# Splitting the first block's loads over two DMA queues in a fused attention and feed-forward kernel

## The chip, the cores and the metric

The kernel runs on one core of a Trainium2 chip. The metric is the device time of one execution in microseconds. TensorE (PE) multiplies matrices, VectorE (DVE), ScalarE (ACT) and GpSimd (POOL) work element by element, and SyncE (SP) issues DMAs. ACT can issue DMAs too, from its own queue, in the order of its other instructions. Each engine takes its instructions in order.

## The reference

```python
def _attn_ref(q, k, v):                      # 4 x 8 heads x 576 x 64
    scores = scale * np.matmul(q, k.transpose(0, 1, 3, 2))
    rel = pos[:, None] - pos[None, :]
    mask_local = (rel >= 0) & (rel < stride)           # heads 0 to 3, stride 32
    mask_strided = (rel >= 0) & (pos[None, :] % stride == pos[:, None] % stride)   # heads 4 to 7
    scores = np.where(masks[None, :, :, :], scores, -1000000000.0)
    ...                                      # softmax over the keys
    return np.matmul(attn, v)

def _moe_ref(x, w_gate, w_val, w_out, rms_g):          # x 2304 x 512, d_ff 1536
    xn = x / rms * rms_g
    g = xn @ w_gate
    silu = g * (1.0 / (1.0 + np.exp(-g)))
    return silu * (xn @ w_val) @ w_out

def _moe2_ref(x, w_a, w_b, w_out):
    return (x @ w_a) * (x @ w_b) @ w_out
```

The output is `_moe2_ref` of `_moe_ref` of the attention's output.

## The kernel before

**Tiling.** The 576 positions are cut into 6 blocks of 96, so a block has 4 x 96 = 384 rows of the feed-forward input. For each block t the attention makes the input (four tiles xx of 128 channels x 384, each a hi part and a lo part in fp32r, so that three matmuls, hi x hi, hi x lo and lo x hi, stand for one in full precision). Then 12 chunks fc of 128 hidden units follow: 12 matmuls into g_ps, 12 into v_ps (L481 to L483), the gate on DVE and ACT, a hi and a lo part of the hidden tile (hl, L506 and L507), and 12 matmuls into y. Block t + 1's attention runs on DVE, ACT and POOL beside block t's matmuls. After block 5 the second feed-forward network follows (L854 to L925).

**Weights.** They come from DRAM as 64-bit words, 512 KB for each third of a chunk (gate, value, out), into tiles gv_raw. A conversion makes 32-bit floats of them: two steps on ACT (L137 and L142) and one on DVE (L145, out cz), all called words steps here, then a hi cast on ACT and a lo subtraction on DVE or POOL (L150 and L151). `convert1(fc)` converts a chunk's gate and value thirds, and all this is done during block 0 alone; later blocks load the converted out weights again.

**Block 0's attention.** Heads 0 to 3 are local: scores on PE (qk, L296), mask (smask, L314), row maximum (lmax, L323), exponentials on ACT (lexp, L336), normalisation (lnorm, L348), transposes (pt, L358) with copies on ACT (ptc, L368), product with the values (pv, L378). They go in three groups 0, 1, 2. Heads 4 to 7 are strided: products on POOL (sqk, L248) that DVE sums (L251), a small softmax (ssub, sexp, snorm), products with the values on POOL (spv, L281), again summed by DVE (L284). POOL has two buffers for its products. pvc and xstc make xx and the squares (L387, L432, lo part L389), rms and rinv the norm. Twenty matmuls on idle data (WARM) and 36 later ones keep PE at work ahead of the first real ones.

**What sets the order.** `LOADS0` and `STEPS0` are lists of names that are called one after the other; a scheduler then orders each engine's instructions, keeping to dependences and to `tc.issue_after` bounds. `GATES` names, for the conversion of chunk 0, 1, 2, 3 and all later ones, which steps of block 0 it has to be issued after (pvr is a sum over values, snorm the strided normalisation, xhi and xlo the last hi and lo part of xx). A DMA waits for its semaphore lane; there are eight, used in turn. All input loads of the kernel before are issued by SP.

Of the kernel before, what the change touches and what calls it, by code (L numbers as in the profile page):

```python
# [37 lines left out]

LOADS0 = "la0 lq ls0 cst la1 lb0 lvl1 lb1 lvl0 lv0"
STEPS0 = ("sqk00 sqk01 sqk02 qk0 qk1 qk2 smask0 lmax0 lexp0 smask1 lmax1 lexp1 smask2 ssub sexp "  # L40
# [5 lines left out]
         "norm pvm snorm sqr",  # L46
         "pvr snorm xhi",
         "snorm sqr sqrt xhi",
# [28 lines left out]
@with_exitstack  # L77
def fused_kernel(ctx: ExitStack, tc: tile.TileContext, qtl, ktl, vl, qs, ks, vs, cst, w1, w2, out):

# [107 lines left out]
    def attention(t, pool, psum, banks):  # L187
# [4 lines left out]
        st = {}  # L192
        steps = {}

        def bank():
# [5 lines left out]
        def load_local(hf, first=False):  # L201

            def f():
                q_t = st["q", hf] = pool.tile([128, 8 * PB], F32, tag="q", name="q_t", bufs=2)
                k_t = st["k", hf] = pool.tile([128, 4, 128], F32, tag="k", name="k_t", bufs=2)
                n = 512 if first else 8 * PB
                nc.sync.dma_start(q_t[:, :n], qtl[t, hf, :, :n])
                nc.sync.dma_start(k_t, ktl[t, hf])
            return f

        def load_rest(hf):
            def f():
                nc.sync.dma_start(st["q", hf][:, 512:], qtl[t, hf, :, 512:])
            return f
# [10 lines left out]
        def load_q():  # L225
            q_t = pool.tile([128, 4, 3, D], F32, tag="qx", name="qs_t", bufs=1)
            nc.sync.dma_start(q_t, qs[:, :, 3 * t:3 * t + 3, :])
            st["qs"] = q_t
# [3 lines left out]
        def load_kv(src, key, g):  # L232
            def f():
                k_t = pool.tile([128, KX], F32, tag="kv", name="kv_t", bufs=KB)
                k_t = k_t[:, :G * L * D].rearrange("p (g n d) -> p g n d", g=G, d=D)
                nc.sync.dma_start(k_t, src[:, heads(g), :L, :])
                st[key, g] = k_t
# [185 lines left out]
        def sqrt_set():  # L423

            with tc.issue_after(st["exp"].ins):
                nc.scalar.activation(scr, eps_sb, AF.Sqrt)
# [88 lines left out]
    const1 = cpool.enter_context(tc.tile_pool(name="const1", bufs=1))  # L515
    cst_sb = const1.tile([128, 388], F32, name="cst_sb")
    ident = cst_sb[:, 0:128]
    mask_a = cst_sb[:, 128:320].rearrange("p (a k) -> p a k", a=2)
    mask_b = cst_sb[:64, 320:384].rearrange("p (a k) -> p a k", a=1)
    g_sb = cst_sb[:, 384:388]  # L520
    pts = [const1.tile([128, 4, 2, PB], F32, name=f"pt{hf}") for hf in range(2)]
# [46 lines left out]
    s0 = attention(0, pool, psum, itertools.cycle(["att", "y0", "y1", "y2", "y3"]))  # L568
    s0["cst"] = lambda: nc.sync.dma_start(cst_sb, cst)
    for n in LOADS0.split():  # L570
        s0[n]()
    load_units(NFC)
    load_late([(NFC - 4, 2), (NFC - 3, 2)])
# [410 lines left out]
def _layout(inputs):  # L984
# [17 lines left out]
    def st(a):  # L1002
        return a[:, 4:].reshape(B, 4, NM, W, D)
    r["qs"] = c(st(q).transpose(0, 3, 1, 2, 4).reshape(128, 4, NM, D))
    r["ks"] = c(st(k).transpose(0, 3, 1, 2, 4).reshape(128, 4, NM, D))
    r["vs"] = c(st(v).transpose(0, 3, 1, 2, 4).reshape(128, 4, NM, D))

    def ok(rows, n):
        i, j = np.arange(rows)[:, None] % (rows // 2), np.arange(n)[None, :]
        return (j > i) & (j <= i + W), j  # L1010
    cst = np.zeros((128, 388), np.float32)
    cst[:, 0:128] = np.eye(128)
    m, j = ok(128, 96)
    cst[:, 128:224] = np.where(m & (j >= W), BIG, NEG)
    cst[:, 224:320] = np.where(m, BIG, NEG)
    cst[:64, 320:384] = np.where(ok(64, 64)[0], BIG, NEG)
    cst[:, 384:] = np.asarray(inputs["moe_rms_g"]).reshape(NCC, 128).T
    r["cst"] = cst

# [25 lines left out]
```

## Time and profile before

| | us |
|---|---|
| median of 3 runs | 964.13 |
| range of the runs | 962.64 to 965.04 |
| the profiled execution | 965.19 |
| its span, first to last instruction | 963.4 |
| PE busy in the span | 936.9 (97%) |
| DVE, ACT, POOL busy | 624.8, 421.7, 541.8 |

PE's busy time is a share of the span, and says that it is seldom idle. Where it is idle is read from the stretches; what it waits for there, from its waits; and why that comes late, from the timelines of the other engines, following at each step what ended the idle time before an instruction. The granted clock of PE is 1 at 2.4 GHz and 0.5 at 1.2 GHz.

### The profile page before, as it was taken

The page shows a single profiled execution, that of the slowest core. Times are in us where ns is not written, and L with a number is a line of the kernel's source. Part 1 is how long each engine was busy: PE and PEld are TensorE (multiplying, and loading weights), DVE is VectorE, ACT ScalarE, POOL GpSimd, SP SyncE. Part 2 cuts the span into 40 slices and gives each one's busy share as a digit, 9 for nine tenths or more (in the row PEclk, how much of TensorE's full clock was granted, in tenths as well). Part 3 has the DMA queues.
Part 4 walks back from the last instruction along what each step waited for, and adds up shares of the span by engine and source line. Part 5 has one row for each costly group of instructions (what it writes and reads, how often), then busy time and mean ns, then how long its engine had stood idle before and what let it go on. Part 6 is the DMA issues. An engine that isn't in the chain of part 4 may idle for free.

```text
span 963.4 us, 14134 instructions
## 1 busy us (share of the span) xinstructions
PE 936.9 (97%) x5324; PEld 889.0 (92%) x5324; DVE 624.8 (65%) x913; ACT 421.7 (44%) x792; POOL 541.8 (56%) x407
## 2 busy tenths in 40 slices
PE   5998999999999999999999999999999999999998
PEld 4798999999999999999999898999999999999997
DVE  5669867548818895987566378667655655464534
ACT  5987655334433433444555455435425422122110
POOL 3568946458749687969379545654734424123211
PEclk6899999999999999999999999999999999999999
DMA  9964375426534553532788975997993973753701
GB/s 344 408 258 157 110 281 195 159 99 215 175 105 149 174 179 111 177 129 66 270 332 307 358 267 202 369 422 278 359 383 118 341 295 131 290 235 147 259 31 66
DMA packets 57507, 215.55 MB, mean 224 GB/s; under 512 B 5984, under 2 KB 14816, under 8 KB 51808
## 3 DMA queue, kind: packets, MB, share of 16 engines
q1 hardware_dynamic: 57296, 214.53, 61.0%
q8 instruction: 42, 0.69, 0.3%
q14 instruction: 25, 0.20, 0.1%
q10 hardware_dynamic: 144, 0.13, 0.0%
HBM read 172.17 MB, written 42.47 MB: 223 GB/s over the span
## 4 chain that ended last, share of the span: by engine, by line
PE 65%; DVE 7%; POOL 6%; DMA 5%; ACT 4%; issue 4%; SPq 0%; DVEq 0%; ACTq 0%; POOLq 0%
PE o L925 5%; PE o L923 5%; PE o L924 5%; POOL prod L248 4%; DMA raw<-in_w 4%; PE Y L856 4%; PE Y L855 4%; PE Y L854 4%; PE y L482 3%; PE Z L856 3%; PE Z L855 3%; PE Z L854 3%; PE y L483 3%; PE X L854 3%; PE X L856 2%
## 5 line engine op out<-in xcount | busy, mean ns | idle before, releaser
L151 POOL TENSOR_TENSOR hl<-c,hl 128x384 fp32r<-128x384 f32 x72 | 77.4, 1076 | 180.2 <-ACT hl L150 173.6
L248 POOL TENSOR_TENSOR prod<-kv_t,qs_t 128x512 f32<-128x512 f32 (+12 forms) x57 | 107.3, 1903 | 21.5 <-DMA wo<-wod 9.7
L482 PE MATMUL y<-hl,wo 128*128 128x384 f32 x288 | 98.3, 345 | 4.8 <-DVE hl L507 3.7
L281 POOL TENSOR_TENSOR prod<-kv_t,S_t 128x512 f32<-128x512 f32 (+12 forms) x57 | 86.8, 1536 | 22.5 <-issue 8.2
L481 PE MATMUL v_ps<-xx,gv 128*128 128x384 f32 x288 | 97.2, 337 | 1.9 <-DVE sg L760 1.9
L481 PE MATMUL g_ps<-xx,gv 128*128 128x384 f32 x288 | 97.6, 339 | 0.6 <-DVE sg L764 0.6
L482 PE MATMUL v_ps<-xx,gv 128*128 128x384 f32 x288 | 97.6, 339 | 0.0
L483 PE MATMUL v_ps<-xx,gv 128*128 128x384 f32 x288 | 97.2, 338 | 0.0
L483 PE MATMUL g_ps<-xx,gv 128*128 128x384 f32 x288 | 97.1, 337 | 0.0
L482 PE MATMUL g_ps<-xx,gv 128*128 128x384 f32 x288 | 96.8, 337 | 0.0
L861 DVE TENSOR_TENSOR c<-c,Y 128x384 f32<-128x384 f32 x108 | 58.9, 550 | 58.0 <-PE Y L856 53.6
L483 PE MATMUL y<-hl,wo 128*128 128x384 f32 x288 | 95.4, 340 | 0.0
L507 POOL TENSOR_TENSOR hl<-h,hl 128x384 fp32r<-128x384 f32 x60 | 64.9, 1081 | 51.1 <-ACT hl L506 51.0
L284 DVE TENSOR_REDUCE xs_t<-prod 128x64 f32<-128x448 f32 (+17 forms) x57 | 85.9, 1521 | 10.5 <-POOL prod L281 9.4
L481 PE MATMUL y<-hl,wo 128*128 128x384 f32 x288 | 83.7, 342 | 3.7 <-ACT hl L506 2.1
L924 PE MATMUL o<-slab,hl 128*128 128x512 f32 x214 | 83.7, 392 | 0.0
L923 PE MATMUL o<-slab,hl 128*128 128x512 f32 x214 | 83.7, 392 | 0.0
L925 PE MATMUL o<-slab,hl 128*128 128x512 f32 x214 | 82.5, 394 | 0.0
L150 ACT CAST hl<-c 128x384 fp32r<-128x384 f32 x72 | 37.0, 514 | 94.9 <-DVE c L891 94.6
L856 PE MATMUL Y<-slab,form 128*128 128x384 f32 x216 | 73.1, 338 | 0.0
L855 PE MATMUL Y<-slab,form 128*128 128x384 f32 x216 | 73.0, 338 | 0.0
L854 PE MATMUL Y<-slab,form 128*128 128x384 f32 x216 | 73.0, 338 | 0.0
(148 smaller groups left out, 2463.5 us busy)
## 6 DMA issues: line engine op xcount, KB each, us to landing
form<-formd SPq DMA_DIRECT2D x32, 1792.0 KB, 10.6
wo<-wod SPq DMA_DIRECT2D x60, 512.0 KB, 4.1
raw<-in_w SPq DMA_DIRECT2D x40, 512.0 KB, 7.2
gv_raw<-in_w SPq DMA_DIRECT2D x32, 512.0 KB, 10.1
formd<-form SPq DMA_DIRECT2D x6, 1792.0 KB, 7.5
formd<-forms SPq DMA_DIRECT2D x6, 1792.0 KB, 12.5
slab<-x2d SPq DMA_DIRECT2D x24, 384.0 KB, 4.0
wod<-wo SPq DMA_DIRECT2D x12, 512.0 KB, 3.2
```

What stands on the lines that cost most here:

```text
L248: nc.gpsimd.tensor_tensor(pr, st["ks", g][:, :, :n, :], st["qs"][:, heads(g), mm:mm + 1, :].to_broadcast([128, G, n, D]), op=ALU.mult)
L281: st["pvm"] = nc.gpsimd.tensor_tensor(pr, st["vs", g][:, :, :n, :], st["S"][:, heads(g), mm, :n, None].to_broadcast([128, G, n, D]), op=AL ...
L284: st["pvr"] = nc.vector.tensor_reduce(st["xs"][:, mm, heads(g), :], pr.rearrange("p g n d -> p g d n"), axis=X, op=ALU.add)
L481: nc.tensor.matmul(out_ps, w_hi, x_hi, start=start, stop=False)
L482: nc.tensor.matmul(out_ps, w_hi, x_lo, start=False, stop=False)
L483: nc.tensor.matmul(out_ps, w_lo, x_hi, start=False, stop=stop)
L854: nc.tensor.matmul(bank(n), hi, x[p][:, 0, c], start=begins and c == 0, stop=False, skip_group_check=not begins)
L855: nc.tensor.matmul(bank(n), hi, x[p][:, 1, c], start=False, stop=False, skip_group_check=not begins)
L856: nc.tensor.matmul(bank(n), lo, x[p][:, 0, c], start=False, stop=c == 1, skip_group_check=not begins)
L923: nc.tensor.matmul(o, h[:, 0, cols], w[0], start=n == 0, stop=False)
L924: nc.tensor.matmul(o, h[:, 0, cols], w[1], start=False, stop=False)
L925: nc.tensor.matmul(o, h[:, 1, cols], w[0], start=False, stop=n == len(chunks) - 1)
```

## The change

Block 0's loads go into two queues: SP keeps q, the strided queries (qs), the values and the weights, and ACT issues the local keys, the masks, the strided keys (ks), the rest of q's second half and the identity. The constants are split into masks (with the gains, 260 columns) and the identity (128 columns). The first chunk's gate and value thirds (`w0`) are issued ahead of the values. The strided queries, keys and values of block 0 get arrays of their own, in which a partition's data is contiguous. The table that prepares the square root is also to be issued after the strided exponentials. The gate of chunk 2 gets xlo.

```diff
-LOADS0 = "la0 lq ls0 cst la1 lb0 lvl1 lb1 lvl0 lv0"
+LOADS0 = "la0 masks lq ls0 la1 lb0 lb1 w0 cst lvl1 lv0 lvl0"
...
-         "pvr snorm xhi",
+         "pvr snorm xhi xlo",
...
+        second = nc.scalar if t == 0 else nc.sync
...
-                nc.sync.dma_start(k_t, ktl[t, hf])
+                second.dma_start(k_t, ktl[t, hf])
...
-                nc.sync.dma_start(st["q", hf][:, 512:], qtl[t, hf, :, 512:])
+                (second if hf else nc.sync).dma_start(st["q", hf][:, 512:], qtl[t, hf, :, 512:])
...
-            nc.sync.dma_start(q_t, qs[:, :, 3 * t:3 * t + 3, :])
+            nc.sync.dma_start(q_t, qs[t])
...
-                nc.sync.dma_start(k_t, src[:, heads(g), :L, :])
+                if t == 0:
+                    (second if key == "ks" else nc.sync).dma_start(k_t, {"ks": ks0, "vs": vs0}[key])
+                else:
+                    nc.sync.dma_start(k_t, src[:, heads(g), :L, :])
...
-            with tc.issue_after(st["exp"].ins):
+            with tc.issue_after(st["exp"].ins), tc.issue_after(st["sexp"].ins):
                 nc.scalar.activation(scr, eps_sb, AF.Sqrt)
...
-    cst_sb = const1.tile([128, 388], F32, name="cst_sb")
+    cst_sb = const1.tile([128, 128], F32, name="cst_sb")
+    mask_sb = const1.tile([128, 260], F32, name="mask_sb")
...
-    s0["cst"] = lambda: nc.sync.dma_start(cst_sb, cst)
+    s0["masks"] = lambda: nc.scalar.dma_start(mask_sb, masks)
+    s0["cst"] = lambda: nc.scalar.dma_start(cst_sb, cst)
+    s0["w0"] = lambda: load_units(1)
...
-    load_units(NFC)
+    load_units(NFC - 1)
```

What the scheduler makes of it shows at three places. (Line numbers of the new file are 4 to 8 higher: its L340 is L336 of before, L372 is L368, L268 is L264, L391 is L387, L436 is L432, L511 is L507, L783 is L776, L785 is L778, L767 is L760.)

ACT, from the program's start, before:

```order
L336 ACT_TABLE_LOAD
L336 ACTIVATE s_t,lsm<-s_t,lmx 128x96 x8
L137 ACTIVATE gv_raw<-gv_raw 128x512
L142 ACTIVATE cz<-gv_raw 128x512
L368 COPY pt_114<-att 96x8x64
L264 ACTIVATE S_t<-S_t 128x12x3
```

and after:

```order
L209 DMA k_t<-in_ktl 128x512
L574 DMA mask_sb<-in_masks 128x260
L238 DMA kv_t<-in_ks 128x768
L209 DMA k_t<-in_ktl 128x512
L214 DMA q_t<-in_qtl 128x256
L575 DMA cst_sb<-in_cst 128x128
L340 ACT_TABLE_LOAD
L340 ACTIVATE s_t,lsm<-s_t,lmx 128x96 x4
L137 ACTIVATE gv_raw<-gv_raw 128x512
L142 ACTIVATE cz<-gv_raw 128x512
L340 ACTIVATE s_t,lsm<-s_t,lmx 128x96 x4
L137 ACTIVATE gv_raw<-gv_raw 128x512
```

Six DMA issues stand ahead of the table load, and the first third's words steps have moved from behind the second group's exponentials to between the first and the second group's. (The fifth issue waits for the lane of the first, the sixth for that of the masks.)

ACT, around chunk 1's conversion and the first scalings of xx, before:

```order
L142 ACTIVATE cz<-gv_raw 128x1024
L387 ACTIVATE xx<-att,cst_sb 128x384
L432 ACTIVATE sq<-att 128x384
L150 CAST gv<-cz 128x2x512
L387 ACTIVATE xx<-att,cst_sb 128x384
L432 ACTIVATE sq<-att 128x384
L387 ACTIVATE xx<-att,cst_sb 128x384 x2
L137 ACTIVATE gv_raw<-gv_raw 128x1024
```

and after:

```order
L142 ACTIVATE cz<-gv_raw 128x1024
L391 ACTIVATE xx<-att,mask_sb 128x384
L436 ACTIVATE sq<-att 128x384
L391 ACTIVATE xx<-att,mask_sb 128x384
L436 ACTIVATE sq<-att 128x384
L150 CAST gv<-cz 128x2x512
L391 ACTIVATE xx<-att,mask_sb 128x384 x2
L137 ACTIVATE gv_raw<-gv_raw 128x1024
```

The cast of chunk 1 has moved behind the second scaling and its square.

DVE, ahead of the lo part of chunk 5's hidden tile, before:

```order
L778 SCALAR_TENSOR_TENSOR v_ps<-th,v_ps 128x384
L760 SCALAR_TENSOR_TENSOR sg<-g_ps,rinv 128x384
L346 TENSOR_SCALAR lsm<-lsm 64x8
L347 RECIPROCAL lrs<-lsm 64x8
L348 TENSOR_TENSOR s_t<-s_t,lrs 64x512
L251 TENSOR_REDUCE S_t<-prod 128x2x6
L776 TENSOR_TENSOR v_ps<-sg,v_ps 128x384
L145 SCALAR_TENSOR_TENSOR cz<-gv_raw,cz 128x1024
L260 TENSOR_REDUCE smx<-S_t 128x12
L507 TENSOR_TENSOR hl<-v_ps,hl 128x384
```

and after:

```order
L350 TENSOR_SCALAR lsm<-lsm 64x8
L351 RECIPROCAL lrs<-lsm 64x8
L145 SCALAR_TENSOR_TENSOR cz<-gv_raw,cz 128x1024
L352 TENSOR_TENSOR s_t<-s_t,lrs 64x512
L767 SCALAR_TENSOR_TENSOR sg<-g_ps,rinv 128x384
L785 SCALAR_TENSOR_TENSOR v_ps<-th,v_ps 128x384
L145 SCALAR_TENSOR_TENSOR cz<-gv_raw,cz 128x512
L255 TENSOR_REDUCE S_t<-prod 128x2x6
L783 TENSOR_TENSOR v_ps<-sg,v_ps 128x384
L511 TENSOR_TENSOR hl<-v_ps,hl 128x384
```

The words step of 1024 columns has moved from straight ahead of the lo part to seven places ahead, with one of 512 columns behind it, and the gate's last step for this chunk (v_ps<-th,v_ps) has moved closer to the lo part.

## Rows read from the trace of the kernel before

**Rows 1.** Stretches: start:end and length in us; PE, PEld, DVE, ACT, POOL busy; clock, DMA.

```profile
0.00:6.00 6.00, 4.95 (x25) 3.77 (x26) 0.26 (x3) 1.28 (x1) 1.62 (x6) 1.00 0.64 187
9.00:29.50 20.50, 12.80 (x82) 10.20 (x83) 15.46 (x34) 15.30 (x38) 10.48 (x8) 0.50 1.03 407
...
40.00:53.50 13.50, 10.06 (x52) 8.61 (x52) 8.91 (x14) 13.47 (x19) 5.63 (x3) 1.00 1.04 405
...
88.00:91.00 3.00, 0.06 (x1) 0.00 (x0) 3.00 (x3) 1.21 (x3) 1.83 (x1) 1.00 0.27 109
91.00:94.50 3.50, 2.94 (x9) 2.94 (x10) 3.50 (x8) 2.41 (x7) 0.73 (x1) 0.51 0.70 214
...
131.50:963.40 831.90, 823.56 (x4653) 784.84 (x4651) 530.61 (x769) 323.41 (x607) 459.12 (x353) 1.00 0.60 219
```

**Rows 2.** Issue and landing of the first raw weights.

```profile
L111 SPq DMA_DIRECT2D gv_raw<-in_w x1: 581/581/581, 8.2 to 8.2; - x1
...
DMA to landing us min/median/max: 6.3/6.3/6.3
```

**Rows 3.** Timeline of DVE, first 16 us: start, duration, instruction, idle time before it.

```profile
8.25 0.56 DVE L314 SCALAR_TENSOR_TENSOR s_t<-att,cst_sb 128x384 f32<-128x384 f32 x1 [7.17 <-DMA cst_sb<-in_cst]
...
12.36 0.56 DVE L314 SCALAR_TENSOR_TENSOR s_t<-att,cst_sb 128x384 f32<-128x384 f32 x1 [2.05 <-PE att L296]
```

**Rows 4.** Timeline of PE, 5 to 25 us.

```profile
5.29 1.23 PE L296 MATMUL att<-k_t,q_t 128*128 128x96 f32 x8
10.34 3.89 PE L296 MATMUL att<-k_t,q_t 128*128 128x96 f32 x24 [3.82 <-DMA k_t<-in_ktl]
```

**Rows 5.** Timeline of ACT, 9 to 52 us.

```profile
13.54 0.37 ACT L336 ACTIVATE s_t<-s_t,lmx 128x96 f32<-128x96 f32 x1 [2.37 <-DVE lmx L323]
...
14.99 0.64 ACT L137 ACTIVATE gv_raw<-gv_raw 128x512 f32<-128x512 f32 x1
...
16.84 0.58 ACT L368 COPY pt<-att 96x512 f32<-96x512 f32 x1 [0.65 <-PE att L358]
...
18.10 1.28 ACT L426 ACT_TABLE_LOAD   x1
...
25.75 1.14 ACT L142 ACTIVATE cz<-gv_raw 128x1024 uint32<-128x1024 uint16 x1
...
29.29 1.04 ACT L150 CAST gv<-cz 128x1024 fp32r<-128x1024 f32 x1 [1.42 <-DVE cz L145]
...
35.21 0.88 ACT L432 ACTIVATE sq<-att 128x384 f32<-128x384 f32 x2
...
51.43 0.46 ACT L506 CAST hl<-v_ps 128x384 fp32r<-128x384 f32 x1
```

**Rows 6.** Timeline of POOL, 7 to 24 us.

```profile
19.03 1.96 POOL L281 TENSOR_TENSOR prod<-kv_t,S_t 128x256 f32<-128x256 f32 x2 [7.67 <-DVE S_t L273]
22.01 2.46 POOL L281 TENSOR_TENSOR prod<-kv_t,S_t 128x768 f32<-128x768 f32 x1 [1.02 <-DVE xs_t L284]
```

**Rows 7.** Timeline of DVE, 18 to 30 us.

```profile
20.73 0.81 DVE L145 SCALAR_TENSOR_TENSOR cz<-gv_raw,cz 128x512 uint32<-128x512 uint32 x1 [0.72 <-ACT cz L142]
...
21.57 0.36 DVE L284 TENSOR_REDUCE xs_t<-prod 128x256 f32<-128x256 f32 x1
```

**Rows 8.** ACT's one DMA issue, at the kernel's end: duration in ns, start.

```profile
L918 ACTq DMA_DIRECT2D out_dram<-slab x1: 377/377/377, 960.7 to 960.7; - x1
```

**Rows 9.** PE's waits, 33 to 150 us: releaser, us in total, times, longest.

```profile
PE y L482 <- DVE hl L507: 3.7, 2, 3.5
PE v_ps L481 <- DVE sg L760: 1.9, 2, 1.0
PE y L481 <- ACT hl L506: 1.4, 1, 1.4
```

**Rows 10.** Timeline of DVE, 80 to 92 us.

```profile
87.83 3.08 DVE L145 SCALAR_TENSOR_TENSOR cz<-gv_raw,cz 128x1024 uint32<-128x1024 uint32 x1
...
90.97 0.54 DVE L507 TENSOR_TENSOR hl<-v_ps,hl 128x384 fp32r<-128x384 f32 x1
```

More of the change, by code (lines that the diff above doesn't have):

```diff
@@ L77, in fused_kernel @@
 @with_exitstack
-def fused_kernel(ctx: ExitStack, tc: tile.TileContext, qtl, ktl, vl, qs, ks, vs, cst, w1, w2, out):
+def fused_kernel(ctx: ExitStack, tc: tile.TileContext, qtl, ktl, vl, qs, ks, vs, ks0, vs0, masks, cst, w1, w2, out):
     nc = tc.nc
@@ L515, in fused_kernel @@
     const1 = cpool.enter_context(tc.tile_pool(name="const1", bufs=1))
-    cst_sb = const1.tile([128, 388], F32, name="cst_sb")
[L517 to L520, printed above, removed]
+    cst_sb = const1.tile([128, 128], F32, name="cst_sb")
+    mask_sb = const1.tile([128, 260], F32, name="mask_sb")
+    ident = cst_sb
+    mask_a = mask_sb[:, 0:192].rearrange("p (a k) -> p a k", a=2)
+    mask_b = mask_sb[:64, 192:256].rearrange("p (a k) -> p a k", a=1)
+    g_sb = mask_sb[:, 256:260]
     pts = [const1.tile([128, 4, 2, PB], F32, name=f"pt{hf}") for hf in range(2)]
@@ L1003, in st @@
         return a[:, 4:].reshape(B, 4, NM, W, D)
-    r["qs"] = c(st(q).transpose(0, 3, 1, 2, 4).reshape(128, 4, NM, D))
+    r["qs"] = c(st(q).transpose(0, 3, 1, 2, 4).reshape(128, 4, NB, NM // NB, D).transpose(2, 0, 1, 3, 4))
     r["ks"] = c(st(k).transpose(0, 3, 1, 2, 4).reshape(128, 4, NM, D))
     r["vs"] = c(st(v).transpose(0, 3, 1, 2, 4).reshape(128, 4, NM, D))
+    r["ks0"], r["vs0"] = (c(r[n][:, :, :NM // NB]) for n in ("ks", "vs"))
     def ok(rows, n):
@@ L1010, in ok @@
         return (j > i) & (j <= i + W), j
-    cst = np.zeros((128, 388), np.float32)
-    cst[:, 0:128] = np.eye(128)
+    cst = np.zeros((128, 260), np.float32)
     m, j = ok(128, 96)
[L1014 to L1018, printed above, removed]
+    cst[:, 0:96] = np.where(m & (j >= W), BIG, NEG)
+    cst[:, 96:192] = np.where(m, BIG, NEG)
+    cst[:64, 192:256] = np.where(ok(64, 64)[0], BIG, NEG)
+    cst[:, 256:] = np.asarray(inputs["moe_rms_g"]).reshape(NCC, 128).T
+    r["masks"] = cst
+    r["cst"] = np.eye(128, dtype=np.float32)
     def weights(a, b, o):
```

## The prediction

> **What bounds the kernel now.** I read the stages first [rows 1]: the reader is to see that TensorE (PE) is the bound almost everywhere. From 131.5 us to the end it is busy 823.56 of 831.90 us, and past some 200 us the instructions of PE, ACT, DVE and POOL stand in the same order in both programs. So the change can pay only in what stands ahead: the attention of block 0 up to the first real matmul, and the first block's 12 chunks, in which ACT, DVE and POOL convert weights while PE works. Three stretches of [rows 1] show where PE loses time there: 9.00 to 29.50 (12.80 of 20.50 busy, at half clock, 1.2 GHz), 40.00 to 53.50 (10.06 of 13.50) and 88.00 to 91.00 (0.06 of 3.00). PE's waits [rows 9] name the releasers of the last two: sg on DVE, the first hi copy on ACT, and 3.7 us for a lo part on DVE. In 40.00 to 53.50 ACT is busy 13.47 of 13.50 us: there ACT's queue is the bound, and whatever lets ACT reach that stretch sooner moves PE by as much.
>
> Then I followed the chain back from there. ACT's pair of squares (35.21) stands behind a cast that waited 1.42 us for DVE, and that behind the words step at 25.75 [rows 5], which starts when POOL frees a buffer: POOL's third value product at 22.01 [rows 6]. That one waited 1.02 us for a DVE reduce (21.57), which stood behind a words step that had waited 0.72 us for ACT [rows 7]. The first value product (19.03) waited for the strided softmax, which hangs on the local one: DVE idles 7.17 us for the constants [rows 3], PE 3.82 us for the second keys [rows 4], ACT 2.37 us for the second row maximum [rows 5].
>
> **The change part by part.** *Masks.* They leave the large constant load and become the second DMA of ACT's queue. That issue falls at 0.73 plus one issue of 0.38 [rows 8], so about 1.1. The constants were issued at 3.0 and let DVE go at 8.25 [rows 3], 5.2 later; with the same 5.2 the masks are there at 6.3 at the latest, before PE has the first scores (5.29 + 1.23 = 6.52 [rows 4]). So PE becomes the releaser: the first mask step at 6.6 rather than 8.25, a gain of 1.65.
>
> *ACT as an issuer.* Six issues of 0.38 [rows 8] are 2.3 us, and the sixth (the identity) waits for the masks, so ACT is held until about 6.3 + 0.4 = 6.7; behind it is queued ACT's first table load, 1.28 as the later one took [rows 5], ready at 8.0. The first exponentials need the row maximum at 6.6 + 1.18 = 7.8 (mask to exponential took 13.54 - 12.36 = 1.18 [rows 3, 5]). So issuing costs 0.2 of the 1.65; without that cover it would be the whole 3.6.
>
> *Second keys and first raw weights.* The keys are issued fourth on ACT, near 1.9, rather than seventh on SP. Before, PE was let go at 10.34 [rows 4]. The bytes ahead of them are nearly the same, so their gain is what idle DMA time is filled: DMA was busy 64% of the first 6 us [rows 1], 2.2 us idle, and 103% afterwards. Bounds 8.1 and 10.3; I take 9.0, since the first queued transfers are what two issuers fill. PE needs 2.0 us for them (10.34 to 12.36), so the second mask step comes at 11.0 (10.1 to 12.3). DVE's new order puts the first normalisation (0.56, as the like-sized step of [rows 3]) ahead of the second maximum: second exponentials at 11.0 + 0.56 + 1.18 = 12.7 (11.9 to 14.0) for 13.54. ACT's order puts two conversion steps of 0.64 [rows 5] between the first and second exponentials, in the 2.37 us that it waited. They need the first raw weights: before, issued at 8.2, landed 6.3 later at 14.5 [rows 2]; now 960 KB fewer stand ahead, 2.4 us at the 407 GB/s of [rows 1], so 12.1 at the latest and, with all idle time filled, 9.9. I take 11.0: ACT is through at 12.3 and holds nothing. Gain at the second exponentials 0.8 (-0.5 to 1.6). The values move behind the weights: they land about 14, needed at 17.8.
>
> *From there to POOL.* The same steps follow in both orders. The second pair of conversion steps stands where the first pair stood. ACT's wait for PE before its copy (0.65 [rows 5], of which I take 0.4) goes, since the first normalisation is done long before: the first value product at 17.8 for 19.03, gain 1.2. The third product's 1.02 us of waiting shrinks, as the reduce no longer stands behind a words step that waits for ACT, but stands behind three of them: about 0.5 less. Gain 1.7 at the words step of 25.75.
>
> *ACT's order around the first cast.* Now two scalings and two squares stand ahead of the cast, where one of each stood: about 0.9 of the 1.42 us wait is filled (two squares take 0.88 [rows 5], and a scaling has a square's shape). Gain 2.6 at 35.21. The gate on the third chunk (xlo) puts the last two lo parts of the input ahead of the chunk's words steps on DVE; ACT's words steps are late enough (over 1 us behind the scalings) that DVE has time for them: nothing, and a cost of up to 1.1 (the two lo steps, 2 x 0.56) if that cover is gone.
>
> *ACT's order in the bound stretch.* One conversion step of 0.64 now stands ahead of the first hi copy (51.43 [rows 5]), which PE waits for [rows 9]: -0.6. Gain 2.0 (0.7 to 2.8).
>
> *The 3.7 us stall stays.* DVE's steps ahead of that lo part are the same set in another order, and PE stands at the same point of its own work there (96 + 84 + 64 matmuls). So it moves with the rest. After it PE is never idle until 131.5, and the end moves with it.
>
> I deduct 0.1 for PE's squares, which now stand apart. Sum: -1.65 + 0.2 + 0.65 (what DVE's order and the second keys give back, from 1.45 to 0.8) - 0.4 - 0.5 - 0.9 + 0.6 + 0.1 = **-1.9 us**. Against the profiled execution, 965.19 (span 963.4 and 1.8 around it), that is 963.3; that execution lies 1.06 above the median of the runs, so I predict 964.13 - 1.9 = **962.2**.
>
> **The rivals.** (a) *The second queue brings nothing but order.* If the transfers ahead arrive no sooner, second keys come at 10.3, second exponentials at 14.0, 0.5 later than before, the gain at 25.75 falls to 0.4, and at the end to 0.6: **963.5**. For it: DMA is at 103% from 9 us on [rows 1]; against it: the 64% before 6 us. The Trainium skill, "DMA: Bandwidth & Descriptors", section "Issuing engines are not separate DMA queues", says that DMAs of several issuers run on the same 16 engines and that a second issuer saves only issue time, which stands for this case; the row's idle third in the first 6 us speaks against it, and no run here yet shows two queues.
> (b) *The stall at 88 goes.* Before, a words step that took 3.08 us stood straight ahead of the lo part [rows 10]; now other steps do. If that wait vanishes, 3.5 us and half of the 3.5 us at 1.2 GHz that follow it [rows 1], 1.7, come on top: **957.0**; with half the wait gone and no fall of the clock, 1.75 + 1.7 more, **958.7**. Against: DVE's total ahead of the lo part is unchanged, and the words step is slow beside POOL, whose work is unchanged too.
> (c) *Slower: ACT held by the raw weights.* ACT takes its queue in order; the second exponentials now stand behind a step that waits for 512 KB. They come at landing + 1.3, and the end moves by (that - 13.54) less 1.1 (0.4 + 0.5 + 0.9 - 0.6 - 0.1). It turns slower when they land after 13.3. If the two queues share so that they land at 15.5, 1 us after the old time: 16.8 - 13.54 - 1.1 = +2.2, **966.3**. Against: only 12.1 by the bytes ahead.
>
> **How the numbers follow.** Forecast 0.57, (a) 0.16, (b) 0.20, (c) 0.07. The forecast is the likeliest, 962.2, with its own range of 961.4 to 963.5. The range that should hold 8 in 10 reaches into half of (b) and up to the near side of (c): 958.6 to 965.2. About 0.3% is what a measurement of this kernel can tell from no change, 2.9 us: below 961.2 lie (b) and 0.04 of the forecast's edge, 0.23 in all (a little of (b) misses it); above 967.0 some of (c) and orders that go wrong unseen, 0.05; within, 0.72.
>
> **What would show it.** Right: first mask step at 6.5 to 6.8, released by PE; second exponentials near 12.7; first value product near 17.8; words step of the second chunk near 24; ACT busy without a break from about 35.5; the 3 us stall on DVE's lo part near 86; PE's stretch from the second block on unchanged. Wrong: ACT idle on a raw weight between the exponentials (c), the words step of the second chunk after 25 (a), no stall near 86 (b), or a new stall of PE in the first block, which no step here has.

## The result, and the profile after

The changed kernel takes 969.43 us (median of 6 runs, 968.31 to 969.82). The kernel before, run beside it, has 962.35 (6 runs, 961.0 to 965.04). The ratio is 1.0067, 95% interval 1.0052 to 1.0083: about 6.5 us **slower** (7.1 by the medians). The forecast was 962.2, with a range of 958.6 to 965.2, and 5% for slower.

| | before | after |
|---|---|---|
| median, us | 962.35 | 969.43 |
| profiled execution, us | 965.19 (a second one: 962.7) | 969.41 |
| its span, us | 963.4 (960.9) | 967.5 |
| granted clock, mean of the span | 0.986 (0.991) | 0.989 |
| PE, DVE, ACT, POOL busy, us | 936.9, 624.8, 421.7, 541.8 | 937.4, 631.1, 423.6, 538.9 |

The profiled execution of before that the prediction rests on lies 2.8 us above its median, while that of after lies at its median. So before was profiled once more (below, "The kernel before, profiled again"), in an execution of 962.7 us, and what stands behind the first 60 us is compared with that one. DVE is the engine whose busy time grew most, by 6.3 us (5.4 against the second profile).

**The start went as forecast.** The timelines of the changed kernel (start, duration, instruction, idle time before it) begin with what the load part of the change was to bring. First DVE, ACT and PE up to 13 us; these answer to [rows 3 to 5]:

```profile
6.68 0.56 DVE L318 SCALAR_TENSOR_TENSOR s_t<-att,mask_sb 128x384 f32<-128x384 f32 x1 [5.59 <-PE att L300]
```

```profile
8.05 0.38 ACT L340 ACTIVATE s_t<-s_t,lmx 128x96 f32<-128x96 f32 x1
...
10.57 0.68 ACT L137 ACTIVATE gv_raw<-gv_raw 128x512 f32<-128x512 f32 x1 [0.98 <-DMA gv_raw<-in_w]
...
12.74 0.38 ACT L340 ACTIVATE s_t<-s_t,lmx 128x96 f32<-128x96 f32 x1 [0.94 <-DVE lmx L327]
```

```profile
8.66 3.73 PE L300 MATMUL att<-k_t,q_t 128*64 128x64 f32 x24 [2.02 <-DMA q_t<-in_qtl]
```

The first mask step comes at 6.68 and waits for PE, no longer for the constants (8.25 before). The second exponentials come at 12.74 (13.54 before). In between ACT waits 0.98 us for the raw weights, which land at 10.55, and this holds up nothing, since the second row maximum comes later still.

**Then the gain is lost in two places.** The stages of the changed kernel (start:end and length; PE, PEld, DVE, ACT and POOL busy; clock, DMA):

```profile
43.70:47.00 3.30, 3.30 (x12) 3.30 (x12) 2.18 (x5) 3.29 (x6) 2.45 (x1) 0.51 1.03 401
...
60.00:94.50 34.50, 31.31 (x185) 29.44 (x184) 31.77 (x47) 25.77 (x63) 26.77 (x15) 0.95 0.41 145
94.50:131.50 37.00, 34.79 (x217) 32.69 (x216) 26.28 (x34) 21.60 (x37) 25.95 (x17) 1.00 0.24 89
131.50:205.00 73.50, 70.12 (x433) 66.69 (x434) 48.88 (x80) 34.85 (x79) 40.38 (x37) 1.00 0.60 208
205.00:959.00 754.00, 750.63 (x4206) 716.17 (x4205) 484.22 (x687) 294.59 (x535) 420.07 (x318) 1.00 0.61 222
```

and of the kernel before, in its second profile:

```profile
43.70:47.00 3.30, 3.22 (x19) 2.83 (x17) 2.20 (x5) 3.29 (x6) 2.06 (x1) 1.00 1.03 402
...
60.00:94.50 34.50, 32.77 (x207) 31.78 (x206) 30.41 (x49) 27.26 (x64) 31.02 (x17) 1.00 0.45 154
94.50:131.50 37.00, 34.23 (x212) 31.48 (x211) 31.46 (x38) 25.21 (x43) 25.43 (x17) 1.00 0.44 151
131.50:205.00 73.50, 73.45 (x463) 71.60 (x462) 43.13 (x76) 29.71 (x75) 43.27 (x39) 1.00 0.58 190
205.00:959.00 754.00, 748.77 (x4186) 712.25 (x4184) 485.36 (x690) 291.77 (x530) 415.53 (x315) 1.00 0.61 222
```

Read PE's busy time. From 205 us on the two agree (750.63 and 748.77 of 754): nothing is lost there. In 60.00 to 94.50 PE is busy 1.46 us less after the change and the clock falls to 0.95, and in 131.50 to 205.00 it is busy 3.33 us less, though before it was all but fully busy there. In between, from 94.50 to 131.50, nothing is lost (34.79 for 34.23). The same, told by how late PE is: I counted its main matmuls from the first real one on (12 into g_ps, 12 into v_ps, and so on) and took the time of each against the one with the same number in the second profile of before. The changed kernel is 1.61 us *early* at the first, 1.62 late when 48 are done, 0.54 late with 96, 5.15 with 240, 8.07 with 672, and 7.19 with 2500. So about 3 us go between the first real matmul and the third chunk, of which 1 comes back, and some 7 us go between 60 and 205 us. That second part is the result. In the first part, a piece is the clock: from 43.70 to 47.00 PE has 12 matmuls at 0.51, where before it has 19 at 1.00. A wait of 3.15 us on sg stands ahead of it (1.22 us in the second profile of before).

PE's waits from 60 to 205 us (releaser; us in total, times, longest), after:

```profile
PE y L485 <- ACT wo L150: 3.6, 4, 1.6
PE g_ps L485 <- DVE sg L767: 2.3, 3, 1.0
PE att L362 <- DVE s_t L352: 1.1, 1, 1.1
PE g_ps L485 <- DVE sg L771: 0.9, 1, 0.9
```

and before, second profile:

```profile
PE y L482 <- DVE hl L507: 2.1, 2, 1.7
PE g_ps L481 <- DVE sg L764: 0.9, 1, 0.9
```

The one stall on a lo part (3.5 us in the first profile [rows 9], 1.7 in the second) became four shorter ones on an out weight's hi cast and four on sg, of which one (0.9 us) stood there before. With the short rows left out here, the waits are 8.5 us for 4.4.

### The profile page after: what moved, and what is told of

Read it like the earlier page. It is cut to its first block, busy times and chain, and to the rows that moved or that the text cites. A ratio compares the mean times of both kernels' runs of the same rounds, so it can differ in the third digit from the quotient of the medians.

```text
span 967.5 us, 14133 instructions
## 1 busy us (share of the span) xinstructions
PE 937.4 (97%) x5324; PEld 888.3 (92%) x5324; DVE 631.1 (65%) x913; ACT 423.6 (44%) x794; POOL 538.9 (56%) x407
## 4 chain that ended last, share of the span: by engine, by line
PE 69%; DMA 9%; DVE 8%; POOL 5%; issue 4%; ACT 3%; SPq 0%; DVEq 0%; POOLq 0%; ACTq 0%
PE o L932 5%; PE o L931 5%; PE o L930 5%; PE Y L863 4%; PE Y L862 4%; PE Y L861 4%; DMA gv_raw<-in_w 3%; DMA raw<-in_w 3%; POOL prod L252 3%; PE y L486 3%; PE y L485 3%; PE g_ps L487 3%; PE y L487 3%; PE v_ps L487 3%; PE v_ps L486 3%
## 5 line engine op out<-in xcount | busy, mean ns | idle before, releaser
L486 PE MATMUL y<-hl,wo 128*128 128x384 f32 x288 | 96.8, 342 | 1.1 <-POOL hl L511 1.0
L511 POOL TENSOR_TENSOR hl<-h,hl 128x384 fp32r<-128x384 f32 x60 | 64.7, 1078 | 54.4 <-ACT hl L510 54.4
L487 PE MATMUL y<-hl,wo 128*128 128x384 f32 x288 | 92.7, 335 | 0.0
L485 PE MATMUL y<-hl,wo 128*128 128x384 f32 x288 | 84.1, 344 | 6.1 <-ACT wo L150 3.6
```

The lines of the kernel that those rows point to most:

```text
L485: nc.tensor.matmul(out_ps, w_hi, x_hi, start=start, stop=False)
L486: nc.tensor.matmul(out_ps, w_hi, x_lo, start=False, stop=False)
L487: nc.tensor.matmul(out_ps, w_lo, x_hi, start=False, stop=stop)
```

## Experiments

"Held to an order" means: for PE, ACT, DVE and POOL a table gives the order of their instructions from where the two kernels part after block 0's attention (about 61 us) to 205 us, and an edge between neighbours keeps the scheduler to it; in the earlier part and in SP's issues it is free. The work is the same, the DMAs and gates are those of the kernel named. The traces show the orders as meant, with one exception: in the changed kernel held to the old order, and in the one with the loads alone, POOL does one out weight's lo part behind two products, where the old order has it ahead of them (in the loads alone, products at 64.68 and lo part at 68.42).

### The gate taken out, the gate alone

Two kernels: the changed one without its new gate, and the kernel before with it.

```diff
-         "pvr snorm xhi xlo",
+         "pvr snorm xhi",
```

> The changed kernel with its gate on the third chunk as before (xlo taken out of it); the loads stay changed, and from the fourth chunk on every engine keeps the changed kernel's order. Theory O (order: what costs time is the other order of block 1's attention steps among the chunks' steps from about 61 us on, which a scheduler chose after the loads changed; the gate costs only the 2.3 us in which ACT waits at 34 for DVE's lo step): first sg step near 40.9 rather than 42.2, but the stalls of PE after 85 stay, 967 to 969.5. Rival G (the gate alone is the cause, all the later delay follows from the step at 34): 962 or less, no PE stall at 110 to 118. Rival D (data: the loads land in another order and the later stretch waits for them, whatever the order of instructions): 967 to 969.5 as O.

> The kernel before with the gate on the third chunk alone. From the fourth chunk on every engine keeps the order of before. Theory O: DVE's lo step for the third chunk waits for ACT's squares (35.2 + 0.9), so the cast at 35.95 comes near 38.5 and the first sg step 2 to 2.6 us later than 42.08; at the end 963.5 to 965 against 962.35. Rival G: all of the 7 us, 969. Rival D: as O, 962.4 to 965.

Measured: without the gate 969.25 us, ratio to the kernel before 1.0063 (1.0043 to 1.0084); the gate alone 964.88, 1.0013 (0.9998 to 1.0028). So the gate is not what makes the changed kernel slow, in the order that it has. By itself it costs 1.3 us by the ratio, with an interval that reaches nothing. The traces show what it does. ACT and DVE around the first cast, after:

```profile
33.27 0.84 ACT L436 ACTIVATE sq<-att 128x384 f32<-128x384 f32 x2
36.44 1.05 ACT L150 CAST gv<-cz 128x1024 fp32r<-128x1024 f32 x1 [2.33 <-DVE cz L145]
37.91 0.58 ACT L452 ACTIVATE rms_t<-att,eps_sb 128x384 f32<-128x384 f32 x1
```

```profile
33.77 1.14 DVE L393 SCALAR_TENSOR_TENSOR xx<-att,mask_sb,xx 128x384 fp32r<-128x384 f32 x2 [4.56 <-ACT sq L436]
34.83 1.83 DVE L145 SCALAR_TENSOR_TENSOR cz<-gv_raw,cz 128x1024 uint32<-128x1024 uint32 x2
```

and the same places with the gate alone:

```profile
38.52 1.05 ACT L150 CAST gv<-cz 128x1024 fp32r<-128x1024 f32 x1 [2.01 <-DVE cz L145]
```

```profile
36.15 1.14 DVE L389 SCALAR_TENSOR_TENSOR xx<-att,cst_sb,xx 128x384 fp32r<-128x384 f32 x2 [3.87 <-ACT sq L432]
```

The lo parts of xx on DVE wait 4.56 us (3.87) for ACT's squares, though a square isn't their operand: both read the same accumulator tile att, and in this order the lo part comes behind. The gate puts DVE's words steps (L145) behind the lo parts, and ACT's cast behind those. ACT stands idle for 2.33 us (2.01), and the norm (rms_t) comes at 37.91, where before it came at 37.92. So by the norm the whole 2 us that the loads had gained are gone. Without the gate ACT is held by PE there instead, for 1.97 us:

```profile
37.33 0.58 ACT L452 ACTIVATE rms_t<-att,eps_sb 128x384 f32<-128x384 f32 x1 [1.97 <-PE att L440]
```

since PE's sums of squares now stand behind matmuls that it could start sooner (two of them at 34.95, two at 36.48, while the last squares are done at 33.90). So 0.6 us of the 2 us is all that the gate takes from the norm; most of the rest goes with those sums. The 969.25 us is in theory O's range and in rival D's, which the next two kernels tell apart.

### The new loads in the old order, and the old loads in the new order

```diff
+ORDER = {"PE": [...], "Activation": [...], "DVE": [...], "Pool": [...]}   # the other kernel's, 61 to 205 us
...
+for row in ORDER.values():
+    for first, then in zip(row, row[1:]):
+        tc.add_manual_dep(tc.nc.find_inst_by_name(f"I-{then}"), f"I-{first}", edge, ...)
```

> The changed kernel, loads and gate and all, but PE, ACT, DVE and POOL are held to the order of the kernel before from the point at which the two orders part (PE from 61 us, DVE from 60, ACT from 60, POOL from 36) to where they meet again near 205 us. Only edges between instructions of one engine are added. Theory O: PE is 1.4 us ahead of before at 60 us and keeps most of it, 960.5 to 962.5. Rivals G and D: the later stretch stays slow, 967 to 970.

> The mirror image: the kernel before, with its own loads and without the gate, but PE, ACT, DVE and POOL held to the order of the changed kernel from where the orders part (61 us) to where they meet (205 us). Theory O: 5.5 to 8 us slower than before, 968 to 970.5, with PE stalls on sg near 111 and on wo near 118 as in the changed kernel. Rivals G and D: as before, 961.5 to 963.5.

Measured: the changed kernel in the old order 964.71, ratio 1.0020 (1.0006 to 1.0035); the kernel before in the new order 972.31, 1.0093 (1.0073 to 1.0113). This settles the main question. **The order alone makes the kernel before as slow as the changed one, and more**, and the old order gives the changed kernel 0.47 of its 0.67% back. Both lie outside theory O's ranges: 964.71 is 2 us above 960.5 to 962.5, so PE's lead at 60 us was not kept (PE waits 3.5 us for a lo part on DVE in this profile), and 972.31 is 2 us above 968 to 970.5. PE's waits of the kernel before in the new order, 60 to 205 us, are led by those of the changed kernel:

```profile
PE y L481 <- ACT wo L150: 3.8, 4, 1.6
PE g_ps L481 <- DVE sg L760: 2.9, 3, 1.6
```

### The kernel before, profiled again

No edit.

> The kernel before once more, unchanged, for a second profile. Its first profiled execution took 965.2 us where most take 962 to 963, at a mean clock of 0.986 where most have 0.990. Theory: the difference is the 3.5 us stall of PE at 88 and the 3.4 us at 1.2 GHz that follow it, which a usual execution does not have: then a profile of 961 us span shows a stall of at most 1.8 us there and no fall of the clock. Rival: the difference lies elsewhere, and the stall is there in full.

Measured: 962.7 us, and the stall near 86 us is 1.73 us, not 3.5, as the theory had it. Its waits and stages are shown above. DVE's words step straight ahead of the lo part, in this execution:

```profile
85.92 1.21 DVE L145 SCALAR_TENSOR_TENSOR cz<-gv_raw,cz 128x1024 uint32<-128x1024 uint32 x1
```

and POOL beside it:

```profile
85.79 3.58 POOL L151 TENSOR_TENSOR gv<-cz,gv 128x1024 fp32r<-128x1024 f32 x1
```

The same instruction of the same program took 3.08 us at 87.83 in the first profile [rows 10]. There it began 1.84 us after POOL's lo part of gv, which ran from 85.99 for 3.84, and ended 1.08 behind it. Here it began within 0.13 us of POOL's, took 1.21, and POOL's step (3.58) ended 2.24 us behind it. So the 3.7 us that the prediction took over as a fixed stall is not a property of the program alone: it depends on how far POOL's step has got when DVE comes to that point. The fall of the clock behind it is seen in the first profile only (0.51 from 91.0 to 94.5 [rows 1]; 1.00 from 87.8 to 91.0 in the second).

### Which part of the loads is worth something

Three kernels without the gate and held to the old order: the changed loads; the same list of loads with all of them issued by SP; and the first raw weights back behind the values.

```diff
-        second = nc.scalar if t == 0 else nc.sync
+        second = nc.sync
...
-    s0["masks"] = lambda: nc.scalar.dma_start(mask_sb, masks)
-    s0["cst"] = lambda: nc.scalar.dma_start(cst_sb, cst)
+    s0["masks"] = lambda: nc.sync.dma_start(mask_sb, masks)
+    s0["cst"] = lambda: nc.sync.dma_start(cst_sb, cst)
```

```diff
-LOADS0 = "la0 masks lq ls0 la1 lb0 lb1 w0 cst lvl1 lv0 lvl0"
+LOADS0 = "la0 masks lq ls0 la1 lb0 lb1 cst lvl1 lv0 lvl0 w0"
```

> The changed kernel without its gate on the third chunk, and with PE, ACT, DVE and POOL held to the order of the kernel before from where the orders part to where they meet (205 us): what is left of the change is the loads alone. Theory O: ACT's wait at 34 is gone, the first sg step comes near 41 (before 42.08), the 1.1 to 1.5 us are kept to the end, 960.5 to 962. Rival F (full queues: PE waits in the stretch 40 to 54 and near 88 for DVE and ACT, which have the same work to do whatever starts earlier, and eat the gain): 962 to 963.5. Rival D (the changed transfers cost time later): 963.5 to 965, as with the gate.

> As loads_only_order_before, but every load is issued by SP in the same new sequence: one queue of issues. If the second queue does what the prediction says (it fills the idle transfer time of the first 6 us), the second keys land some 1.3 us later than with two queues, the second exponentials come near 14.0 rather than 12.7, and the end is 1 to 1.5 us later than loads_only_order_before, 962 to 963.5. Rival: the second queue brings nothing, same time and same landing within 0.3 us.

> As loads_only_order_before, two queues, but the first chunk's raw weights stand behind the values, as before the change. If having them first matters (ACT fills its wait for the second row maximum with two conversion steps), the squares at 33.3 come about 1 us later and the end 0.5 to 1.2 us later than loads_only_order_before. Rival: the weights' place is worth nothing, within 0.3 us.

Measured: the loads alone 963.9, ratio 0.9994 (0.9982 to 1.0007); one queue 960.86, **0.9973 (0.9954 to 0.9992)**; weights behind the values 962.15, 0.9984 (0.9971 to 0.9996). The last two were forecast later than the loads alone and came sooner; the loads alone lie in rival D's range. The version in one queue is the fastest that computes the whole result, ahead of both kernels. Its interval overlaps that of two queues, so I do not claim that the second queue costs time; no run shows that it brings any.

These three can't be read as the price of the loads to 0.2%, though. The loads alone are the kernel in which POOL's order is not quite the old one, and there PE waits 3.5 us for a lo part on DVE, as in the first profile of before; with one queue it waits 1.9 us, with the weights behind the values 1.4, and there POOL's order is the old one. So what the changed loads are worth in the old order lies between 0.06 and 0.27% by these ratios, and only the last two are clear of nothing; the 1.9 us (0.2%) that the prediction gave them are not refuted. PE's second scores, one queue and then two:

```profile
10.26 3.89 PE L300 MATMUL att<-k_t,q_t 128*128 128x96 f32 x24 [3.49 <-DMA k_t<-in_ktl]
```

```profile
8.70 3.29 PE L300 MATMUL att<-k_t,q_t 128*64 128x64 f32 x24 [1.77 <-DMA q_t<-in_qtl]
```

With two queues PE starts 1.56 us sooner, and its last operands are there at 8.87 for 10.13. They were issued at 2.14 for 3.54, and took 6.7 and 6.6 us to land: the lead is time saved in issuing. But the first real matmul stands at 32.10 with two queues and at 31.66 with one: the lead is gone by then. Then ACT's first hi copy, which PE waits for, one queue and then two:

```profile
49.59 0.45 ACT L510 CAST hl<-v_ps 128x384 fp32r<-128x384 f32 x1
```

```profile
51.00 0.49 ACT L510 CAST hl<-v_ps 128x384 fp32r<-128x384 f32 x1
```

The 1.4 us between these two may come from the order ahead of 61 us, which was left to the scheduler and which it draws a little differently in each. So these three differ in that, too, beside their loads and POOL's one step, and which of them makes the 0.2% is not settled.

### Block 1's products on POOL left out

The suspects in the new order were the words steps on DVE beside POOL. Block 1's 12 product steps on POOL, the largest readers there, are replaced by fills of the same tiles, once in the new order (the changed kernel) and once in the old (the kernel before). So the strided half of block 1's attention is not computed in these and in the last experiment. (The expectation says 36 steps; it is 12.) Two of the 12 fills wait for no operand of their own and run far ahead, at 25.93 and 28.28 us in the new order and at 27.08 and 29.41 in the old; the next experiment has all of them behind 60 us.

```diff
-                nc.gpsimd.tensor_tensor(pr, ...)
+                if t == 1:
+                    nc.gpsimd.memset(pr, 0.0)
+                else:
+                    nc.gpsimd.tensor_tensor(pr, ...)
```

> The changed kernel in its own order on PE, ACT, DVE and POOL, but the 36 products of the strided attention of block 1 on POOL are left out: a fill of the same tile stands for each, so POOL writes as many elements but reads nothing (that block's attention is wrong by it). Theory P (what the changed order costs is DVE's words steps standing beside POOL instructions that read: nine 1024- and 512-wide steps take 16.7 us between 60 and 205 us, 13.2 in the order of before): the steps that lay beside products (2.77, 2.71, 2.47 us) fall to 1.2, the stalls at 85 to 90 and 117 shrink, 963.5 to 966.5. Rival Q (only the places in the queues count): the words steps keep their length beside a busy POOL, 968 to 969.5. The Trainium skill, SBUF - State Buffer, section Who interferes with whom, says that a DVE instruction with two SBUF inputs is shut out by a GpSimd instruction that reads SBUF, not by one that only writes it; by that theory P holds.

> The same fills in the kernel before, in its own order. Theory P: its words steps lie beside products less (1.06, 2.02 and 3.17 us at 68, 72 and 100), so it gains less, 0.5 to 2 us: 960.5 to 962.3; the distance between the two orders shrinks from 7 us to 3 to 5. Rival Q: no gain in either, distance 7 us as it was.

Measured: new order 961.73, ratio 0.9986 (0.9974 to 0.9999); old order 958.9, 0.9954 (0.9941 to 0.9968). In the new order the products cost 7.8 us (1.0067 - 0.9986 = 0.81% of 963), in the old 4.4 (0.46%). The distance between the orders shrinks from 6.5 to some 3 us (0.32%). So about half of it is in what POOL's products do, and the other half isn't. Both kernels came out faster than theory P's ranges, by some 2 us.

### More work on POOL, but none that reads

Each of the 12 products is replaced by two fills, so that POOL is busy longer than with one and still has no operand to read. The fills take 15.2 us in all, where the products take 20.7 in the changed kernel.

```diff
-                    nc.gpsimd.memset(pr, 0.0)
+                    nc.gpsimd.memset(pr, 0.0)
+                    nc.gpsimd.memset(pr, 0.0)
```

> As no_products_order_after, but each of the 12 products of block 1 (12, where that run's expectation said 36) is replaced by two fills one behind the other, so POOL is held about as long as by the product (two fills of 0.65 for a product of 1.2 to 1.5 us) and still reads nothing; block 1's strided attention is left out of the result by it. Theory P (DVE's words steps are shut out while POOL reads): the words steps stay short, 10.5 to 12 us for nine, and most of the 7.7 us gained there stays, 961 to 964. Rival T (POOL's time was what counted: shorter fills gave POOL's lo parts and the reduces an earlier start): the gain goes back, 966.5 to 969.5, with words steps short or long.

Measured: 963.7, ratio 0.9999 (0.9987 to 1.0010). Of the 7.8 us that leaving out the products gave, 6.5 stay (1.0067 - 0.9999 = 0.68%; by the medians 5.7). So most of the products' price in this order is not POOL's time, but what reading products do to others. Not all of POOL's time is given back, though: from one fill to two POOL's time grows by 7.6 us and the kernel's by 1.3, and by that the missing 5.5 would be worth another 0.9 or so (an estimate from these runs). Two words steps of this kernel, on DVE:

```profile
80.30 1.22 DVE L145 SCALAR_TENSOR_TENSOR cz<-gv_raw,cz 128x1024 uint32<-128x1024 uint32 x1
...
82.96 2.90 DVE L145 SCALAR_TENSOR_TENSOR cz<-gv_raw,cz 128x512 uint32<-128x512 uint32 x1
```

and POOL beside them:

```profile
80.18 0.74 POOL L254 MEMSET prod<- 128x768 f32 x1
...
82.80 2.52 POOL L151 TENSOR_TENSOR gv<-cz,gv 128x1024 fp32r<-128x1024 f32 x1 [1.87 <-PE v_ps L495]
```

Beside a fill 1024 columns take 1.22 us; beside a lo part, which reads, half as many take 2.90. In the changed kernel itself, DVE:

```profile
82.15 2.71 DVE L145 SCALAR_TENSOR_TENSOR cz<-gv_raw,cz 128x1024 uint32<-128x1024 uint32 x1
...
86.31 2.89 DVE L145 SCALAR_TENSOR_TENSOR cz<-gv_raw,cz 128x512 uint32<-128x512 uint32 x1
...
100.45 0.56 DVE L767 SCALAR_TENSOR_TENSOR sg<-g_ps,rinv 128x384 f32<-128x384 f32 x1
```

POOL:

```profile
81.93 1.85 POOL L252 TENSOR_TENSOR prod<-kv_t,qs_t 128x768 f32<-128x768 f32 x1
86.02 2.64 POOL L151 TENSOR_TENSOR gv<-cz,gv 128x1024 fp32r<-128x1024 f32 x1 [2.24 <-ACT gv L150]
```

and ACT:

```profile
89.24 0.62 ACT L150 CAST wo<-cz 128x512 fp32r<-128x512 f32 x1 [2.33 <-DVE cz L145]
```

The first words step ends 1.08 us after POOL's product (84.86 and 83.78), the second 0.54 after POOL's lo part (89.20 and 88.66): about what each takes alone (1.2 and 0.65). So it looks as if each waits until POOL is through and then runs. Behind the second stands the hi cast of the out weight on ACT (idle 2.33 us for it), and behind that PE: the wait of 1.6 us on wo in the table above. A step that reads an accumulator (sg, 100.45) takes its usual 0.56, though one of POOL's lo parts runs from 98.89 to 101.32.

The nine words steps on gv_raw between 60 and 110 us, by kernel (shortest, median, longest in ns; first and last start). The kernel before, second profile:

```profile
L145 DVE SCALAR_TENSOR_TENSOR cz<-gv_raw,cz x9: 651/1225/3168, 64.5 to 100.4; 128x1024 uint32<-128x1024 uint32 x5, 128x512 uint32<-128x512 uint32 x4
```

The changed kernel:

```profile
L145 DVE SCALAR_TENSOR_TENSOR cz<-gv_raw,cz x9: 678/2237/2887, 64.5 to 105.5; 128x1024 uint32<-128x1024 uint32 x5, 128x512 uint32<-128x512 uint32 x4
```

The kernel before in the new order:

```profile
L145 DVE SCALAR_TENSOR_TENSOR cz<-gv_raw,cz x9: 679/2251/2883, 63.7 to 103.8; 128x1024 uint32<-128x1024 uint32 x5, 128x512 uint32<-128x512 uint32 x4
```

The median is twice as long in the new order, whatever the loads, and with the two fills it is back at 1226. Added up, the nine take 13.2 us before, 16.7 in both kernels with the new order, 12.8 in the changed kernel with the old, 10.6 without products and 12.6 with fills.

The Trainium skill, "SBUF — State Buffer", section "Who interferes with whom", says that an instruction of VectorE with two operands in SBUF and one of GpSimd that reads SBUF exclude each other for their whole length, that GpSimd's fills don't, and that who is issued first decides. The traces here agree: 1.22 us beside a fill, 2.71 and 2.89 beside steps that read, and 1.21 or 3.08 for one and the same step, by whether POOL's was well under way. Who was issued first the rows don't show: POOL's starts 0.13 us ahead in the shorter case, too.

### The gate's first step sooner

If PE's waits on sg were the price of the order, five sg steps placed 3 to 7 places sooner on DVE, in an order otherwise the changed kernel's, would give some of it back. The edit moves five numbers in DVE's row of ORDER.

> The changed kernel in its own order on PE, ACT and POOL; on DVE five sg steps (at 78.21, 85.39, 91.66, 111.09 and 175.37 us of the changed kernel's trace) stand 3 to 7 places earlier, where their product was ready, ahead of the attention's steps. Theory O1 (PE's stalls on sg at 85.1 and 110.7 and before 174.2 are a matter of DVE's queue alone): 1.9 to 3 us back, 966.5 to 967.5. Rival O2 (DVE is full in this stretch, so what stands behind, the words steps for the weights and the lo parts, is late instead): the stalls move to y and wo, 968.5 to 970.

Measured: 970.44, ratio 1.0075 (1.0057 to 1.0094): nothing. PE's waits, 60 to 205 us:

```profile
PE y L485 <- ACT wo L150: 4.3, 3, 2.1
PE y L485 <- ACT hl L510: 1.4, 1, 1.4
PE y L486 <- DVE hl L511: 1.4, 1, 1.4
```

The waits on the gate's first step (L767) are gone, and others stand in their place, on wo and on the hidden tile, as rival O2 had it. So sg was one carrier of DVE's lateness and not its cause. The nine words steps of this kernel:

```profile
L145 DVE SCALAR_TENSOR_TENSOR cz<-gv_raw,cz x9: 674/1219/2752, 64.6 to 105.9; 128x1024 uint32<-128x1024 uint32 x5, 128x512 uint32<-128x512 uint32 x4
```

They take 13.8 us in all and 1.2 in the median, hardly more than before, and the kernel is no faster than with 16.7. So their sum alone doesn't set the time: here they are shorter, but some start later (84.60 and 87.65 us for 82.15 and 86.31), and what waits for them is as late.

## Why the prediction was wrong

**Right: the loads up to 13 us.** First mask step 6.68 (forecast 6.5 to 6.8), released by PE; first exponentials 8.05 (8.0), so the six issues on ACT cost no more than was said; PE's second operands at 8.88 (9.0); raw weights at 10.55 (11.0); second exponentials 12.74 (12.7). Of rival (c) the sign is there, ACT idle for 0.98 us on the raw weights, but not the harm; (a) was to show in the second chunk's words step after 25 us, and that came at 24.64. The way to the 8.88 was another than forecast, though: DMA was busy 0.68 of the first 6 us where before it was 0.64, so little idle time was filled. The keys were issued at 2.13 for 4.13 and took 6.7 us to land.

**Nearly right: up to 35 us.** POOL and one step of DVE, after:

```profile
17.93 2.40 POOL L285 TENSOR_TENSOR prod<-kv_t,S_t 128x256 f32<-128x256 f32 x2 [6.11 <-DVE S_t L277]
...
21.89 1.48 POOL L285 TENSOR_TENSOR prod<-kv_t,S_t 128x768 f32<-128x768 f32 x1 [1.55 <-DVE xs_t L288]
```

```profile
19.35 2.13 DVE L145 SCALAR_TENSOR_TENSOR cz<-gv_raw,cz 128x512 uint32<-128x512 uint32 x2
```

The first value product is there at 17.93 (17.8), 1.1 us sooner than before. But the third's wait grew to 1.55 us where it was to shrink by 0.5 from 1.02 [rows 6]: the reduce that it waits for stands behind two words steps that took 2.13 us beside POOL, 0.5 more than two of the 0.81 of [rows 7], and the pair of products took 2.40 for 1.96. It looks like the effect that the last experiments show. The words step of the second chunk came at 24.64 (about 24; 25.75 before), the squares 1.9 us sooner rather than 2.6, and the first real matmul at 31.80, 1.6 us ahead of the second profile of before.

**Wrong: the gate costs nothing.** It was priced at nothing, or at up to 1.1 us if DVE had no time for the lo parts. DVE had the time (4.56 us idle), but the lo parts wait for ACT's squares. ACT, forecast to be busy from 35.5 on, stands idle until 36.44. The gate's part in the loss is 0.6 us; without it, the norm waits 1.97 us for PE's sums of squares, which the prediction put at 0.1 ("PE's squares, which now stand apart"). The step ahead of the first hi copy was priced rightly at 0.6: the norm comes as early as before, the copy at 51.99 for 51.43. The lead is used up at PE's first v_ps of the second chunk:

```profile
42.81 0.44 PE L485 MATMUL v_ps<-xx,gv 128*128 128x384 f32 x1 [3.15 <-DVE sg L767]
```

It came at 42.42 in the second profile of before. Taking the gate out in the final order changes nothing (1.0063), so what it lost is not the result.

**The step that failed: "the 3.7 us stall stays ... so it moves with the rest. After it PE is never idle until 131.5, and the end moves with it."** It rests on "DVE's steps ahead of that lo part are the same set in another order". That PE is never idle after it was so in the first profile of before alone; in the second it is busy 34.23 of 37.00 us from 94.50 to 131.50. The set's sum was taken as fixed, and the order between 60 and 205 us priced at zero. The order was the result: it costs 0.93% on the loads of before and 0.47% on the new ones. A words step of 1024 columns takes 1.2 us or some 2.7 by whether a reading step of POOL is running when it comes up, so the sum of a set is not the same in another order: 16.7 us for 13.2 over nine steps, and the casts, sg and PE behind them. Of the 7 us, PE's waits account for 4.1 (8.5 - 4.4) and the clock, 0.95 of 34.5 us, for some 1.7 (an estimate); the rest I can't assign to single rows. The clock falls behind the wait of 1.6 us on wo:

```profile
90.00:92.60 2.60, 2.60 (x13) 2.28 (x14) 2.60 (x8) 2.35 (x5) 1.22 (x1) 0.75 0.88 268
92.60:95.80 3.20, 3.20 (x14) 3.20 (x13) 2.34 (x6) 2.98 (x6) 0.00 (x0) 0.67 0.69 277
```

Rival (b) had the place right and the direction wrong. Its argument against, "the words step is slow beside POOL, whose work is unchanged too", held the clue: POOL's work was unchanged, but not what of DVE's ran beside it. "Orders that go wrong unseen" had a part of the 5%; the prediction named "a new stall of PE in the first block" as the sign of it, and that is what the trace shows.

**What stays open.** Without the products the two orders still differ by some 3 us (0.32%), and by which places of the table was not tried beyond the five sg steps. Of the half that goes with the products, the longer words steps are what the traces show; that they make the time is argued, and the last kernel, with words steps as short as before and no gain, shows that more is in it. The fills differ from the products not only in reading: they don't wait for block 1's strided operands or softmax, so a part of their 6.5 us may be that. And the gate's price with the new loads in the old order, 1.0020 against 0.9994, lies at the edge of what the intervals tell apart. What the loads are worth, 0.06 to 0.27% by three ratios, is open.

## What to carry to other kernels

A change of loads in a kernel whose order is drawn by a scheduler is two changes: price the reorder too, and where it touches engines that shut each other out, don't take "the same set of steps" for the same time. To tell the two apart, hold the new kernel to the old order and the old kernel to the new one, and see in the trace that every engine kept it; here that showed that the order made the loss, 0.5 to 0.9%, and that the loads were worth at most some 0.3%. And before a gate is called free, look at what its step waits for, not only at whether its engine has idle time.

## What the runs showed of the hardware

One instruction of one program took 3.08 us in one execution and 1.21 in another, by whether POOL's lo part (3.84 and 3.58 us) had begun well ahead of it; with it a stall of PE went from 3.5 to 1.73 us, and only the longer one was followed by a granted clock of 0.51 (1.2 GHz for most of the 3.5 us). A second issuing engine did land the early loads sooner, 8.87 for 10.13 us, with the issue 1.40 us sooner and as long from issue to landing; no run shows that it was worth anything at the end. And a lo part on DVE that reads the accumulator tile that a square on ACT reads was held back 4.56 us until that square was done; whether the program or the chip makes it wait is open.
